# A routing-attention and gated-FFN kernel: the score matmuls contract over 128 rows of the turned tiles instead of 80

## The chip, the cores and the metric

The kernel runs on one core of a Trainium2 chip. The metric is the device time of one execution in microseconds; before the change, three runs gave 336.65, 339.22 and 339.0 us, with a median of 339.0 us. The profile was taken of one execution, whose span from the first to the last instruction is 336.6 us.

## The reference

Four batches, eight heads, 768 positions, head dimension 64. Queries and keys are each assigned to the nearest of 16 centroids of their head; a query attends only to keys of its own cluster. The attention output of all heads, 512 wide, then goes through a gated feed-forward block.

```
q_assign = argmax(q_n @ c_n);  k_assign = argmax(k_n @ c_n)
mask   = q_assign[..., :, None] == k_assign[..., None, :]
scores = where(mask, (q @ k.T) / 8, -1e9)
attn   = softmax(scores);  y = attn @ v
x      = y as (3072, 512)
out    = (sigmoid(x @ w_gate) * (x @ w_val)) @ w_out      # d_ff = 1536
```

## The kernel before

**The turned tiles.** For each head the fp32 keys and queries are cut into an fp16 high part and an fp16 remainder, the low part. They lie side by side as 128 columns of a tile `hl`: columns 0 to 63 the high parts, 64 to 127 the low parts. `hl` is then transposed into a tile `T` of 128 rows by 12 blocks of 128 positions (six blocks of keys, six of queries), in the first batch and in the first pair of heads of the second by TensorE (lines 637, 720 and 796, copied out of PSUM by VectorE or ScalarE), otherwise by a DMA transpose that SyncE's queue issues (line 319). So rows 0 to 63 of `T` hold high parts and rows 64 to 127 low parts of the 64 dimensions.

**Routing.** The logits `lg` (lines 326 and 335) multiply all 128 rows of each block with a centroid matrix. VectorE takes the maximum and writes one-hot rows; these are turned and put into rows 64 to 79 of `T`, over the low parts of 16 dimensions: by VectorE or ScalarE (lines 681, 685 and 769 to 775) or by small DMAs (line 383). Keys get 1 at their cluster; queries get -1920 at every cluster but their own. One matmul over rows 0 to 79 then gives the score and the mask together.

**A step of attention.** There are 96 steps per batch, 384 in all. In `do_scores` a step multiplies one key block (128 columns, stationary) with three query blocks (384 columns, moving) into a PSUM tile `sc` (line 541), and ScalarE takes the exponential of it into `es` (line 546). In `do_av`, two or three steps later, three matmuls of 65 columns multiply `es` with the values (`av`, line 558). The 65th column of the values is 1 and sums the weights. After the last step of a head VectorE and GpSimd normalise, and the result is turned into `xTb`.

**The order.** The order is written out by hand. Each step issues its `sc`, then pieces of the feed-forward block of an earlier half batch (`ffn_run`; gate `g` at line 397, value `v` at line 412, output `o` at line 429, four matmuls to a piece), then the `av` of an older step, then background work due at this step by the table `SCHED`: casts, splits, turns, logits, loads. TensorE executes in that order. The last feed-forward blocks follow the last step, with no attention beside them. Early in the program, and before some steps, dummy matmuls on a zero tile are issued (lines 538 and 604).

`head_steps` makes the slices of `T` that the score matmul uses. It gives `k` as one block and `q` as three; both begin at row 0.

Of the kernel before, what the change touches and what calls it, by code (L numbers as in the profile page):

```python
# [74 lines left out]
def kernel(  # L75
# [443 lines left out]
    def head_steps(b, p, e, halves):  # L519
        t = T[b, 2 * p + e]  # L520
        steps = []
        order = [(j, i) for j in range(NCH) for i in range(len(halves))]
        for j, i in order:
            for c in halves[i : i + 1]:
                steps.append(dict(
                    b=b, p=p, e=e, nq=3 * len(halves), k=t[0:80, j, :], h0=halves[0],
                    q=t[0:80, 6 + 3 * c : 9 + 3 * c, :], j=j, c0=3 * i,
                ))
        steps[0]["first"] = True
        steps[-1]["last"] = True  # L530
        return steps
# [478 lines left out]
    for b in range(B):  # L1010
        xT = xtp.tile([128, NDC, S], HP, tag="xTb", name="xTb")
        key = min(b, 1)
        for i in range(2):
            u = 96 * b + (96 - 6 * 2 * halved(b) if i == 0 else 96)
            lag = SCHED.get(f"lag{key}{i}", 8)
            if b == B - 1 and i:
                break
            at(u + lag, lambda xT=xT, b=b, i=i: ffn_block(xT, 384 * i, 384, b, CH[i]))
        for p, e, c in heads(b):
            for s in head_steps(b, p, e, c):  # L1020
                s["xT"] = xT
                do_scores(s)
                pend.append(s)
                r = step_no[0] - 96 * b
                ns = SCHED.get(f"ns{b}{r // 24}", SCHED.get(f"ns{b}", 500.0))
                ffn_run(ns if b or r >= 48 else 0.0)
                while len(pend) > LA[min(b, 1)]:
                    do_av(pend.pop(0))
                run_bg(step_no[0])
                step_no[0] += 1  # L1030
# [37 lines left out]
```

## Time and profile before

| | |
|---|---|
| three runs | 336.65, 339.22, 339.0 us; median 339.0 us |
| profiled execution, span | 336.6 us; no other time of that execution is listed |
| instructions | 9001, of them 3422 matmuls and 3422 weight loads |
| TensorE busy | 327.1 us (97%) |
| ScalarE, VectorE, GpSimd busy | 236.4, 187.6, 109.3 us |
| score matmuls `sc` | 384, mean 330 ns |
| mean granted TensorE clock | 0.990 |

A busy time of TensorE counts from the start of a matmul to its modelled end, and matmuls overlap, so how much a matmul costs is better read from the distances between starts. The timeline gives these to a hundredth of a microsecond and merges equal instructions that follow one another.

### The profile page before, as it was taken

The numbers are of one execution on the slowest core, as the hardware profiler recorded it, in microseconds if no ns is written. First come the engines' busy times: TensorE is split into PE (matmuls) and PEld (weight loads), VectorE is DVE, ScalarE is ACT, GpSimd is POOL, SyncE is SP. The second block draws the span as 40 slices with busy tenths as digits, with TensorE's granted clock in tenths as the row PEclk, the third lists the DMA queues.
The fourth block names the chain that finished last, engine by engine and source line by source line (L and its number), as shares of the span: only waits on it lengthen the run. The fifth ranks groups of instructions, "written<-read, shape, count | busy, mean of one in ns | idle before, by whom it ended". The sixth has DMA issues, their size and how long they took to land.

```text
span 336.6 us, 9001 instructions
## 1 busy us (share of the span) xinstructions
PE 327.1 (97%) x3422; PEld 210.8 (63%) x3422; DVE 187.6 (56%) x530; ACT 236.4 (70%) x543; POOL 109.3 (32%) x151
## 2 busy tenths in 40 slices
PE   7798999999999999999999999999999999999996
PEld 4686866766666666666556665666556655654654
DVE  6668755796567777465646664466534331340431
ACT  6587987766899888877768776787777876532321
POOL 6668454442254444513242333313201010100000
PEclk9789999999999999999999999999999999999999
DMA  7999989744795969597457755872622022101002
GB/s 205 360 159 129 204 207 188 105 148 91 239 236 106 229 167 237 148 193 196 90 180 168 189 92 116 234 114 49 130 72 47 14 25 74 46 0 64 32 0 95
DMA packets 80523, 45.25 MB, mean 134 GB/s; under 512 B 57376, under 2 KB 77536, under 8 KB 80480
## 3 DMA queue, kind: packets, MB, share of 16 engines
q1 hardware_dynamic: 74400, 39.83, 49.3%
q0 software_dynamic: 5792, 4.72, 9.9%
q8 instruction: 27, 0.44, 0.6%
q14 instruction: 16, 0.13, 0.1%
q10 hardware_dynamic: 288, 0.13, 0.1%
HBM read 28.34 MB, written 6.29 MB: 103 GB/s over the span
## 4 chain that ended last, share of the span: by engine, by line
PE 86%; DMA 5%; DVE 3%; POOL 2%; issue 2%; SPq 1%; ACT 0%; POOLq 0%; DVEq 0%
PE v L412 18%; PE g L397 18%; PE o L429 17%; PE sc L541 17%; PE av L558 9%; DMA qraw<-in_q_dram 3%; PE lg L335 2%; DMA T<-hl 2%; PE lg L326 1%; PE t_ps L720 1%; POOL hl L708 1%; PE o_end L453 1%; POOL wv L198 1%; PE oh_ps L757 1%; DVE hT L417 1%
## 5 line engine op out<-in xcount | busy, mean ns | idle before, releaser
L546 ACT ACTIVATE es<-sc 128x384 f16<-128x384 f32 x384 | 173.5, 492 | 43.2 <-PE sc L541 26.1
L541 PE MATMUL sc<-T 80*128 80x384 f16 x384 | 118.6, 330 | 0.7 <-DVE T L775 0.2
L558 PEld LDWEIGHTS <-es 128*128 128x128 f16 x1152 | 82.6, 98 | 45.6 <-issue 1.5
L558 PE MATMUL av<-va,es 128*128 128x65 f16 x1152 | 98.1, 194 | 0.0
L417 DVE SCALAR_TENSOR_TENSOR hT<-th,v 128x384 f16<-128x384 f32 x96 | 53.1, 553 | 71.7 <-PE av L558 47.4
L397 PE MATMUL g<-xTb,wg 128*128 128x384 f16 x384 | 78.1, 325 | 0.2
L412 PE MATMUL v<-xTb,wv 128*128 128x384 f16 x384 | 78.1, 325 | 0.0
L429 PE MATMUL o<-wo,hT 128*128 128x512 f16 x276 | 68.7, 378 | 0.0
L299 POOL TENSOR_TENSOR xp<-t,rec 128x192 f16<-128x192 f32 (+1 forms) x46 | 29.1, 633 | 116.7 <-DVE rec L296 76.9
L403 ACT ACTIVATE th<-g 128x384 f32<-128x384 f32 x96 | 47.2, 491 | 25.4 <-DVE hT L417 16.2
L397 PEld LDWEIGHTS <-wg 128*128 128x128 f16 x384 | 37.2, 97 | 21.7 <-issue 1.1
L412 PEld LDWEIGHTS <-wv 128*128 128x128 f16 x384 | 37.2, 97 | 21.0 <-issue 0.7
L429 PEld LDWEIGHTS <-hT 128*128 128x128 f16 x276 | 26.8, 97 | 23.5
L541 PEld LDWEIGHTS <-T 80*128 80x128 f16 x384 | 37.3, 97 | 0.8 <-DVE T L775 0.6
L957 POOL TENSOR_TENSOR hl<-kraw,hl 128x384 f16<-128x384 f32 x22 | 20.4, 927 | 34.4 <-DVE hl L956 18.3
L294 DVE TENSOR_TENSOR t<-av,sv 128x195 f32<-128x195 f32 (+1 forms) x46 | 20.1, 436 | 20.4 <-PE av L558 19.7
L957 POOL TENSOR_TENSOR hl<-qraw,hl 128x384 f16<-128x384 f32 x22 | 20.1, 912 | 21.1 <-DVE hl L956 21.1
L438 ACT ACTIVATE ob<-o 128x512 f32<-128x512 f32 x15 | 9.0, 597 | 12.4 <-PE o L429 12.1
L349 DVE TENSOR_TENSOR lgs<-lg,lglo 128x192 f32<-128x192 f32 x22 | 7.8, 356 | 14.6 <-ACT lglo L341 14.2
L436 DVE TENSOR_SCALAR ob<-o 128x512 f32<-128x512 f32 x8 | 5.5, 690 | 16.8 <-PE o L429 16.8
L248 POOL CAST va<-vraw 128x768 f16<-128x768 f32 x16 | 13.5, 848 | 0.2 <-DMA vraw<-in_v_dram 0.2
L335 PE MATMUL lg<-cm,T 128*128 128x32 f16 x264 | 10.0, 177 | 0.4 <-DMA T<-hl 0.4
(112 smaller groups left out, 248.9 us busy)
## 6 DMA issues: line engine op xcount, KB each, us to landing
vraw<-in_v_dram SPq DMA_DIRECT2D x16, 384.0 KB, 5.4
out_dram<-ob SPq DMA_DIRECT2D x23, 256.0 KB, 2.2
kraw<-in_k_dram SPq DMA_DIRECT2D x15, 384.0 KB, 3.9
qraw<-in_q_dram SPq DMA_DIRECT2D x12, 384.0 KB, 4.1
wg<-in_moe_w_gate_dram POOLq DMA_DIRECT2D x4, 384.0 KB, 5.6
wv<-in_moe_w_val_dram POOLq DMA_DIRECT2D x4, 384.0 KB, 5.8
wo<-in_moe_w_out_dram POOLq DMA_DIRECT2D x2, 768.0 KB, 11.2
qraw<-in_q_dram SPq DMA_DIRECT2D x7, 192.0 KB, 6.8
```

What stands on the lines that cost most here:

```text
L294: DVE.tensor_tensor(t[:, 0:nq, :], av, sv, ALU.add)
L299: (eng or POOL).tensor_tensor(x, t[:, 0:nq, 0:64], bcast(rec[:, 0:nq], 64), ALU.mult)
L335: PE.matmul(out=lg[:, bass.ts(c, 32)], lhsT=t[:, c, :], rhs=cm[:, h].rearrange("p s n -> p (s n)"), start=True, stop=True,)
L397: PE.matmul(out=g[:, 0:n], lhsT=wg[fc // WQ][:, dc, fc % WQ, :], rhs=xT[:, dc, t0 : t0 + n], start=(dc == 0), stop=(dc == NDC - 1),)
L403: ACT.activation(th[:, 0:n], g[:, 0:n], AF.Tanh, scale=0.5)
L412: PE.matmul(out=w[:, 0:n], lhsT=wv[fc // WQ][:, dc, fc % WQ, :], rhs=xT[:, dc, t0 : t0 + n], start=(dc == 0), stop=(dc == NDC - 1),)
L417: DVE.scalar_tensor_tensor(hT[:, fc, 0:n], st[0][:, 0:n], 1.0, w[:, 0:n], ALU.add, ALU.mult)
L429: PE.matmul(out=o, lhsT=hT[:, fc, bass.ts(t, 128)], rhs=wo[fc // 6][:, fc % 6, :], start=(fc == 0), stop=(fc == NFC - 1),)
L541: PE.matmul(out=sc.rearrange("p (c t) -> p c t", t=128), lhsT=s["k"], rhs=s["q"], start=True, stop=True,)
L546: ACT.activation(es, sc, AF.Exp, scale=SCALE)
L558: PE.matmul(out=av[:, s["c0"] + i, :], lhsT=s["es"][:, bass.ts(i, 128)], rhs=VA[b, p][:, e, s["j"], :], start=(first and i == 0), stop=(la ...
L957: POOL.tensor_tensor(hl[:, :, 64:128], r, hl[:, :, 0:64], ALU.subtract)
```

## The change

The slices of `T` that the score matmuls read take in all rows. The key block becomes 128 rows by 128 columns instead of 80 by 128, and the query blocks 128 rows by 384 columns instead of 80 by 384. Rows 80 to 127, which are now read too, hold the low parts of dimensions 16 to 63 of keys and queries, so each score gains the product of these low parts.

```diff
         for j, i in order:
             for c in halves[i : i + 1]:
                 steps.append(dict(
-                    b=b, p=p, e=e, nq=3 * len(halves), k=t[0:80, j, :], h0=halves[0],
-                    q=t[0:80, 6 + 3 * c : 9 + 3 * c, :], j=j, c0=3 * i,
+                    b=b, p=p, e=e, nq=3 * len(halves), k=t[:, j, :], h0=halves[0],
+                    q=t[:, 6 + 3 * c : 9 + 3 * c, :], j=j, c0=3 * i,
                 ))
```

The number and the order of the instructions on every engine, and their waits, are the same in both programs.

## The prediction

> **What bounds the kernel now.** The page is read first: the span, the engines, the granted clock, and the chain that ended last.
>
> ```profile
> span 336.6 us, 9001 instructions
> PE 327.1 (97%) x3422; PEld 210.8 (63%) x3422; DVE 187.6 (56%) x530; ACT 236.4 (70%) x543; POOL 109.3 (32%) x151
> PEclk9789999999999999999999999999999999999999
> PE 86%; DMA 5%; DVE 3%; POOL 2%; issue 2%; SPq 1%; ACT 0%; POOLq 0%; DVEq 0%
> PE v L412 18%; PE g L397 18%; PE o L429 17%; PE sc L541 17%; PE av L558 9%; DMA qraw<-in_q_dram 3%; PE lg L335 2%; DMA T<-hl 2%; PE lg L326 1%; PE t_ps L720 1%; POOL hl L708 1%; PE o_end L453 1%; POOL wv L198 1%; PE oh_ps L757 1%; DVE hT L417 1%
> ```
>
> TensorE carries 86% of the chain, the score matmuls 17% of it. The busy share alone would not prove this, because ends of matmuls are modelled; so the second view is the table of busy times over stretches.
>
> ```profile
> core 0: us, PE busy (x) PEld busy (x) DVE busy (x) ACT busy (x) POOL busy (x), PEclk, DMA share, GB/s
> 40.00:290.00 250.00, 248.86 (x2641) 158.67 (x2642) 145.34 (x404) 194.66 (x453) 82.33 (x105) 1.00 0.64 141
> 290.00:330.00 40.00, 40.00 (x229) 22.25 (x228) 13.10 (x25) 12.57 (x25) 0.51 (x1) 1.00 0.07 25
> ```
>
> From 40 to 290 us TensorE is idle for 250.00 - 248.86 = 1.14 us, while ScalarE, the next engine, has 250 - 194.66 = 55 us to spare. A nanosecond that a score matmul gains or loses there goes to the end one for one, and ScalarE, which takes each `sc`, can follow. So the question is only whether a matmul of 80 rows and one of 128 differ in the time that they hold TensorE.
>
> **What the change removes, adds and moves.** It moves nothing: order, count and waits of instructions stay. On 384 weight loads and 384 matmuls the row count goes from 80 to 128. The groups by line give the nearest rows of both kinds.
>
> ```profile
> L541 PE MATMUL sc<-T 80*128 80x384 f16 x384 | 118.6, 330 | 0.7 <-DVE T L775 0.2
> L397 PE MATMUL g<-xTb,wg 128*128 128x384 f16 x384 | 78.1, 325 | 0.2
> L335 PE MATMUL lg<-cm,T 128*128 128x32 f16 x264 | 10.0, 177 | 0.4 <-DMA T<-hl 0.4
> L397 PEld LDWEIGHTS <-wg 128*128 128x128 f16 x384 | 37.2, 97 | 21.7 <-issue 1.1
> L541 PEld LDWEIGHTS <-T 80*128 80x128 f16 x384 | 37.3, 97 | 0.8 <-DVE T L775 0.6
> ```
>
> *Weight loads.* 97 ns with 80 rows, 97 ns with 128: 384 x 0 = 0. They also lie beside the matmul before them (97 ns of load beside some 160 ns of streaming); if that cover were gone nothing would change, since both kinds take the same.
>
> *Waits.* The low rows of `T` are in place before a score is made: the logits of the same tile, among them the 264 of line 335 above, are made of all 128 rows of it, and the one-hot rows, which come last, follow from those logits. No wait is added, nothing new is queued, and no DMA starts earlier or later but by the shift of TensorE itself.
>
> *Matmuls.* The gate's `g` is the changed `sc` in all that the row shows: 128x128 stationary, 128x384 moving. The means (330 against 325) include modelled ends and the first microseconds, so the distances between starts decide. In the timeline of TensorE I took a stretch of steps with feed-forward pieces between them, and the end of attention, where `av` and `v` stand without an `sc`.
>
> ```profile
> 255.76 0.33 PE L541 MATMUL sc<-T 80*128 80x384 f16 x1
> 255.92 0.81 PE L397 MATMUL g<-xTb,wg 128*128 128x384 f16 x4
> ...
> 271.57 0.33 PE L541 MATMUL sc<-T 80*128 80x384 f16 x1
> ...
> 288.23 0.26 PE L558 MATMUL av<-va,es 128*128 128x65 f16 x3
> 288.32 0.81 PE L412 MATMUL v<-xTb,wv 128*128 128x384 f16 x4
> 288.97 0.35 PE L558 MATMUL av<-va,es 128*128 128x65 f16 x6
> 289.15 0.81 PE L397 MATMUL g<-xTb,wg 128*128 128x384 f16 x4
> ...
> 301.50 0.81 PE L412 MATMUL v<-xTb,wv 128*128 128x384 f16 x4
> ```
>
> Price of a feed-forward piece: from 289.15 to 301.50 stand 19 pieces of four, 12.35 / 19 = 0.650 us, so 162.5 ns for one matmul of 128 rows and 384 columns. Price of three `av`: six take 289.15 - 288.97 = 0.18, so 0.09. Between the `sc` at 255.76 and the one at 271.57 lie 21 `sc`, 21 groups of three `av` and 16 pieces: 15.81 - 16 x 0.650 - 21 x 0.09 = 3.52 us, so 168 ns for an `sc` of 80 rows. It holds TensorE 168 - 162.5 = 5 ns longer than a matmul of 128 rows with the same columns. The rows are rounded to 10 ns, so three `av` take 0.085 to 0.095 and the excess is between 0 and 10 ns.
>
> Against the row count as the reason stands a place where `sc` follows logits:
>
> ```profile
> 154.11 0.46 PE L335 MATMUL lg<-cm,T 128*128 128x32 f16 x12
> 154.42 0.32 PE L541 MATMUL sc<-T 80*128 80x384 f16 x1
> 154.58 0.33 PE L412 MATMUL v<-xTb,wv 128*128 128x384 f16 x1
> ```
>
> Here `sc` has 80 rows too, and the next matmul starts after 0.16 us, as behind a `g`. So the extra may belong to the order (an `sc` behind three short `av`), not to the rows; then it stays.
>
> [...]
>
> *Sum.* In full speed stand
>
> ```profile
> L541 PE MATMUL sc<-T x374: 322/327/337, 20.7 to 287.4; 80*128 80x384 f16 x187
> ```
>
> 374 score matmuls between 20 and 290 us. The two ends are 374 x 0 = 0 and 374 x 10 ns = 3.7 us of gain. A loss per matmul is left out, because `g`, `v` and the weight loads of 128 rows show none. I take the middle, 5 ns: the matmul gets the `g` row's price, 374 x 5 = 1.9 us. The profiled execution's 336.6 us would become 334.7 us. That execution lies by the lowest of the three runs (336.65); the median is 339.0, so the time to forecast is 339.0 - 1.9 = **337.1 us**, 0.6% less. One per cent, 3.4 us, is about what a measurement of this kernel tells from no change.
>
> **The rivals.**
>
> *The extra belongs to the order; nothing changes.* For it: the `sc` behind the logits, and equal weight loads. Against it: the `av` to `v` change at 288.32 shows no extra without an `sc` in it. Time: 339.0 us.
>
> *The whole 10 ns goes, or the early half clock gets shorter.* The stretches at the start, as the trace grants the clock:
>
> ```profile
> 5.87:12.69 6.82, 4.65 (x79) 3.38 (x76) 5.02 (x18) 3.40 (x8) 4.69 (x6) 1.00 1.02 346
> 12.69:19.52 6.83, 6.49 (x68) 5.41 (x69) 2.51 (x10) 5.28 (x11) 4.54 (x6) 0.50 1.13 309
> 26.35:33.17 6.82, 5.59 (x105) 4.53 (x104) 5.55 (x19) 5.41 (x13) 5.53 (x9) 1.00 0.92 130
> ```
>
> After a stretch in which TensorE was busy 4.65 of 6.82 us (68%) it ran 6.83 us at 0.50; after one with 5.59 (82%) it did not. If fuller rows counted as more activity, the half-clock stretch could go, worth up to half of 6.83, 3.4 us. Against it: before 12.69 us only a couple of score matmuls run, some 0.3 us of 6.82, so their rows weigh little. The full 10 ns without that gives 339.0 - 3.7 = 335.3 us.
>
> *A second half-clock stretch; slower.* The place is 26 to 33 us, the next emptiest. [...] The price is at most 3.4 us, as above: 339.0 + 3.4 = 342.4 us. For it: the three runs already lie 2.6 us apart, which one such stretch more or less could make. Against it: the change shortens 26 to 33 us by only about ten matmuls times 5 ns. [...]
>
> *Full rows draw the clock down over the whole attention.* The stretch from 290 to 330 us speaks against it: matmuls of 128 rows without a pause, granted clock 1.00. I give it nothing of its own.
>
> *The change doesn't do what it says.* The slices do reach the instructions, and the products of the low parts add a sum whose size no engine's time depends on; what is left of this rival is the first one.
>
> **How the numbers follow.** 45% for the forecast of 337.1 us (its own range 335.5 to 338.5), 36% for no change (339.0, within 337.5 and 340), 12% for the larger gain (335.3 or less), 7% for a half-clock stretch more (342.4). Faster by over 1% means under 335.6: the larger gain's 12% and a little of the forecast's lower edge, 14%. Slower by over 1% means above 342.4: most of the last case, 6%. The rest, 80%, is within 1%. The range from 334.8 to 340.3 us leaves out the last rival, the lowest part of the larger gain and the upper edge of no change. It takes in the lowest run less 1.9 us.
>
> **What the changed profile would show.** If the forecast holds, the timeline of the same steps has about 0.91 - 0.005 us from `sc` to `sc` with one piece between, and the 21 steps that now take 15.81 us take about 15.70. The groups by line give `sc` near 325 ns, its weight load 97. Idle time of TensorE between 40 and 290 us stays near 1 us, and ScalarE's busy time the same 236 us. If 15.81 stays, the order was the reason. If the weight load grows or the clock row shows less than 1.00 after 20 us, the reasoning about equal rows is wrong. What would make the prediction wrong above all is the start: a half-clock stretch more or less moves the time by more than all 374 matmuls do.

## The result and the profile after

The changed kernel takes 337.16 us (median of 20 runs, 334.37 to 338.82), the kernel before 338.79 us (median of 20 runs, 336.49 to 340.37). The ratio is 0.9956 with a 95% interval of 0.9935 to 0.9976: 0.4% faster, about 1.5 us, and clear of no change. The forecast was 337.1 us against 339.0.

The page of the changed kernel, its first lines and two of its groups:

```profile
span 335.1 us, 9001 instructions
PE 325.0 (97%) x3422; PEld 210.5 (63%) x3422; DVE 186.2 (56%) x530; ACT 235.8 (70%) x543; POOL 109.8 (33%) x151
...
L541 PE MATMUL sc<-T 128*128 128x384 f16 x384 | 117.2, 327 | 0.7 <-DVE T L775 0.2
...
L541 PEld LDWEIGHTS <-T 128*128 128x128 f16 x384 | 37.3, 97 | 0.8 <-DVE T L775 0.6
```

The span falls from 336.6 to 335.1 us. The score matmuls now stand with 128 rows; their mean goes from 330 to 327 ns, and the weight load stays at 97 ns. The span is not the whole time: the profiled execution took 337.21 us, 2.1 us more than its span.

The stretch from 40 to 290 us, and the 40 us without attention:

```profile
40.00:290.00 250.00, 248.83 (x2649) 159.81 (x2646) 144.83 (x405) 194.98 (x455) 83.29 (x106) 1.00 0.64 141
290.00:330.00 40.00, 40.00 (x231) 22.40 (x229) 12.98 (x23) 11.84 (x24) 0.00 (x0) 1.00 0.08 30
```

TensorE is idle for 1.17 us in it (1.14 before), with the clock at 1.00. It is as full as it was, and gets through more matmuls (2649 against 2641 in the same 250 us). That is how the bound engine looks here, with each score step 4 ns shorter. The waits behind this idle time changed a little. From 60 to 290 us the profile lists these for TensorE, in the kernel before and then in the changed one (us in total, times, longest):

```profile
PE lg L335 <- DMA T<-hl: 0.4, 1, 0.4
PE t_ps L637 <- DVE T L685: 0.3, 1, 0.3
```

```profile
PE lg L335 <- DMA T<-hl: 0.7, 2, 0.3
```

One wait of 0.3 us is gone and another has come, 0.7 us in sum both times.

The same 21 steps as in the prediction, in the changed kernel's timeline of TensorE:

```profile
254.38 0.33 PE L541 MATMUL sc<-T 128*128 128x384 f16 x1
254.54 0.81 PE L397 MATMUL g<-xTb,wg 128*128 128x384 f16 x4
...
270.11 0.33 PE L541 MATMUL sc<-T 128*128 128x384 f16 x1
```

They take 270.11 - 254.38 = 15.73 us, against 15.81 before: 0.08 / 21 = 4 ns per step. The trace keeps starts in whole nanoseconds: 15.727 against 15.811 us, and behind a score matmul that follows `av` the next matmul starts after 162 ns instead of 166 (medians of some 260 places). Times 384 steps 4 ns are 1.5 us, as much as the two spans differ.

That this comes out so exactly is in part chance. By the starts of the same score matmuls in the two traces, the changed kernel leads by 0.33 us at the 31st, when 4 ns per step would be 0.12, by 1.09 at the 151st, by 0.67 at the 161st, behind its new wait, by 0.81 at the 201st and by 1.55 at the last. From the 201st on this is 4 ns per step; earlier, the two moved waits and the start add and take some tenths of a microsecond, which cancel in these two executions.

### The profile page after: what moved, and what is told of

It is laid out like the page before. It is cut to its first block, busy times and chain, and to the rows that moved or that the text cites. A ratio compares the mean times of both kernels' runs of the same rounds, so it can differ in the third digit from the quotient of the medians.

```text
span 335.1 us, 9001 instructions
## 1 busy us (share of the span) xinstructions
PE 325.0 (97%) x3422; PEld 210.5 (63%) x3422; DVE 186.2 (56%) x530; ACT 235.8 (70%) x543; POOL 109.8 (33%) x151
## 4 chain that ended last, share of the span: by engine, by line
PE 86%; DMA 6%; DVE 2%; POOL 2%; SPq 2%; issue 1%; ACT 0%; POOLq 0%; DVEq 0%; ACTq 0%
PE o L429 18%; PE v L412 17%; PE g L397 17%; PE sc L541 16%; PE av L558 9%; DMA T<-hl 4%; PE lg L335 2%; DMA qraw<-in_q_dram 2%; PE lg L326 1%; PE t_ps L720 1%; POOL hl L708 1%; PE o_end L453 1%; SPq L163 1%; POOL wv L198 1%; DVE T L731 1%
## 5 line engine op out<-in xcount | busy, mean ns | idle before, releaser
L541 PE MATMUL sc<-T 128*128 128x384 f16 x384 | 117.2, 327 | 0.7 <-DVE T L775 0.2
L541 PEld LDWEIGHTS <-T 128*128 128x128 f16 x384 | 37.3, 97 | 0.8 <-DVE T L775 0.6
```

The costliest lines, as they stand in the source:

```text
L541: PE.matmul(out=sc.rearrange("p (c t) -> p c t", t=128), lhsT=s["k"], rhs=s["q"], start=True, stop=True,)
```

## The experiments

What stays open after the result is why a score matmul of 80 rows costs 4 ns more. The theory of the prediction was only "a matmul of 80 rows holds TensorE longer". Three readings of it are told apart below: the price belongs to each matmul of fewer rows; it belongs to certain row counts (those that leave a group of 32 rows half filled, or a whole group unused; the division into groups of 32 is my supposition, which no trace of this case shows); or it is paid where neighbours in TensorE's order differ in their row count. The measure is the length of the same 21 steps, from the timeline; in the rows, the first and the last `sc` of the 21 are shown. It repeats from execution to execution: three executions with 128 rows, two of the changed kernel and one with a fuller start, give 15.727, 15.726 and 15.727 us, and four with 80, 96 and (twice) 112 rows give 15.811 us each. So one execution of each variant is enough here, and a hundredth of a microsecond counts. The time of one execution is no such measure, because the clock at the start differs between executions (see "The start").

**Other row counts for the score: 96, 112 and 64.**

```diff
-                    b=b, p=p, e=e, nq=3 * len(halves), k=t[0:80, j, :], h0=halves[0],
-                    q=t[0:80, 6 + 3 * c : 9 + 3 * c, :], j=j, c0=3 * i,
+                    b=b, p=p, e=e, nq=3 * len(halves), k=t[0:96, j, :], h0=halves[0],
+                    q=t[0:96, 6 + 3 * c : 9 + 3 * c, :], j=j, c0=3 * i,
```

(and the same with 112 and 64)

> The score matmuls contract over 96 rows, three whole groups of 32, in place of 80 or 128. Measure: the same 21 steps late in the third block of steps (from the score matmul before a gate piece to the 21st score matmul after it), 15.81 us with 80 rows and 15.73 us with 128, so 4 ns per step. Theory 'not the full array' (any row count under 128 beside matmuls of 128 costs): 15.81 us. Theory 'broken group' (a row count that doesn't fill its groups of 32 costs): 15.73 us. Weight load 97 ns in both.

> Score matmuls over 112 rows: four groups of 32 are touched, the last one half filled. Theory 'number of groups' (what costs is that a group of 32 is switched off and on): 15.73 us for the 21 steps, as with 128. Theories 'not the full array' and 'broken group': 15.81 us.

With 96 rows, and then with 112, the timelines have

```profile
252.42 0.33 PE L541 MATMUL sc<-T 96*128 96x384 f16 x1
...
268.23 0.33 PE L541 MATMUL sc<-T 96*128 96x384 f16 x1
```

```profile
254.83 0.33 PE L541 MATMUL sc<-T 112*128 112x384 f16 x1
...
270.64 0.33 PE L541 MATMUL sc<-T 112*128 112x384 f16 x1
```

15.81 us both times, exactly as with 80. Whole groups of 32 (96 rows) don't help, and four groups begun (112 rows) don't either. So neither the half-filled group nor the number of groups is the reason, and the gain doesn't grow with the rows: 32 of the 48 added rows bring nothing.

> Score matmuls over the first 64 rows, so the one-hot rows and with them the mask are left out of the scores. Theory 'not the full array': 15.81 us for the 21 steps, as with 80 rows. Theory 'broken group': 15.73 us. [...]

64 rows are another matter. Two steps of that kernel:

```profile
332.00 0.33 PE L541 MATMUL sc<-T 64*128 64x384 f16 x1
332.27 0.82 PE L397 MATMUL g<-xTb,wg 128*128 128x384 f16 x4
332.93 0.26 PE L558 MATMUL av<-va,es 128*128 128x65 f16 x3
333.12 0.33 PE L541 MATMUL sc<-T 64*128 64x384 f16 x1
...
352.13 0.33 PE L541 MATMUL sc<-T 64*128 64x384 f16 x1
```

From the first `av` to `sc` it now takes 0.19 us instead of 0.09, and from `sc` to the next matmul 0.27 instead of 0.16 or 0.17: about 0.1 us on the way in and 0.1 us on the way out. The 21 steps take 20.13 us, 206 ns per step more than with 80 rows, and the span becomes 421.6 us, 85 us more than before. 384 steps at 206 ns make 79 us of it. The clock, which stands at 0.62 on average over the first 49 us of that kernel, may account for the rest, but that was not separated:

```profile
0.00:49.00 49.00, 45.28 (x422) 27.47 (x422) 23.83 (x86) 25.55 (x54) 25.48 (x43) 0.62 0.74 160
```

What in TensorE takes the 0.1 us each way is not shown. 80, 96 and 112 rows don't pay it: their 21 steps take 15.81 us. Row counts between 64 and 80 were not tried.

**Another matmul with 80 rows: the gate.** The score stays at 128 rows.

```diff
-                        out=g[:, 0:n], lhsT=wg[fc // WQ][:, dc, fc % WQ, :],
-                        rhs=xT[:, dc, t0 : t0 + n],
+                        out=g[:, 0:n], lhsT=wg[fc // WQ][0:80, dc, fc % WQ, :],
+                        rhs=xT[0:80, dc, t0 : t0 + n],
```

> Score matmuls over 128 rows as after the change; the gate matmuls instead contract over the first 80 of the 128 rows of each block, so 48 of 128 terms are left out of the gate. Measure: the stretch behind the last attention step, where pieces of four gate and four value matmuls alternate, 19 pieces in 12.35 us now. Theory 'change of rows' (a fixed price of 4 to 7 ns where the row count changes between neighbours): two changes per gate piece, so 10 gate pieces add 0.07 us: 12.42 us, and within a gate piece the second and third distances stay 162 ns. Theory 'price per matmul' (each matmul of 80 rows holds TensorE 4 ns longer): 10 x 4 x 4 ns = 0.16 us: 12.51 us. If 80 rows cost only in the score's place: 12.35 us.

Behind the last attention step, that kernel's timeline has

```profile
288.93 0.82 PE L397 MATMUL g<-xTb,wg 80*128 80x384 f16 x4
289.59 0.33 PE L412 MATMUL v<-xTb,wv 128*128 128x384 f16 x1
...
301.32 0.33 PE L412 MATMUL v<-xTb,wv 128*128 128x384 f16 x1
```

From the gate piece at 288.93 to the value piece at 301.32 lie 19 pieces, 12.39 us instead of 12.35: 0.04 us over ten gate pieces, 4 ns a piece, although each piece has four matmuls of 80 rows. A price per matmul would have given 0.16 us. In whole nanoseconds the extra stands behind the first matmul of a piece, of a gate piece with 80 rows and of a value piece with 128 alike: 166 to 168 ns, and 161 to 162 behind the other three, as expected. So here a run of equal row counts pays once, going in and coming out, and the place of the score is nothing special. The expected 0.07 us was too much: I had taken up to 7 ns for a change in and out, and it is 4.

**The value matmuls with 80 rows, beside a score of 128 and of 80.**

```diff
-                out=av[:, s["c0"] + i, :], lhsT=s["es"][:, bass.ts(i, 128)],
-                rhs=VA[b, p][:, e, s["j"], :],
+                out=av[:, s["c0"] + i, :], lhsT=s["es"][0:80, bass.ts(i, 128)],
+                rhs=VA[b, p][0:80, e, s["j"], :],
```

> Score matmuls over 128 rows; the three value matmuls of a step contract over the first 80 keys of the 128 of each block, so 48 keys of each block are left out of the sums. Measure: the same 21 steps, 15.73 us with all at 128 rows. Theory 'change of rows': each step has one way into 80 rows and one back, 4 ns in all as with the score: 15.81 us. Theory 'price per matmul': 3 x 4 ns per step: 15.98 us.

> Both the score and the value matmuls contract over 80 rows (48 keys of each block are left out of the sums). Neighbours differ in rows only where a feed-forward piece stands between, 16 times in the 21 steps. Theory 'change of rows': 15.73 us + 16 x 4 ns = 15.79 us, and in the five steps without a piece the next value matmul starts 162 ns after the score, not 166. Theory 'price per matmul': 4 x 4 ns per step, 16.07 us.

The first and last `sc` of the 21 steps, with the score at 128 rows and then at 80:

```profile
253.11 0.33 PE L541 MATMUL sc<-T 128*128 128x384 f16 x1
...
268.91 0.33 PE L541 MATMUL sc<-T 128*128 128x384 f16 x1
```

```profile
253.27 0.33 PE L541 MATMUL sc<-T 80*128 80x384 f16 x1
...
269.05 0.33 PE L541 MATMUL sc<-T 80*128 80x384 f16 x1
```

15.80 us: with the score at full rows and the value matmuls at 80, nearly the whole price is back. 15.78 us: with all four at 80 rows it falls again, though four matmuls instead of one now have fewer rows. Per-matmul prices would have given 15.98 and 16.07; a price per matmul in proportion to its columns, 65 against 384, would have given 15.77 and 15.86, and the second is ruled out. Both lengths are near what a price of 4 ns for each in and out gives (15.81 and 15.79). The second sign that was expected is there too: from a score of 80 rows to a value matmul of 80 rows it is 162 ns, and 166 where only one of the two has 80 (medians over the steps without a piece).

**Twice as many changes.** The score at 80 rows, and of the three value matmuls only the middle one.

```diff
-                out=av[:, s["c0"] + i, :], lhsT=s["es"][:, bass.ts(i, 128)],
-                rhs=VA[b, p][:, e, s["j"], :],
+                out=av[:, s["c0"] + i, :], lhsT=s["es"][0 : (80 if i == 1 else 128), bass.ts(i, 128)],
+                rhs=VA[b, p][0 : (80 if i == 1 else 128), e, s["j"], :],
```

> Score matmuls over 80 rows as before, and of the three value matmuls of a step the middle one over the first 80 keys only (48 keys of every block are left out of one third of the sums), so that the row count changes four times per step and not twice. Theory 'change of rows': the price doubles, 15.73 + 21 x 2 x 4 ns = 15.90 us for the 21 steps. Theory 'price of the score matmul alone': 15.81 us.

```profile
256.44 0.33 PE L541 MATMUL sc<-T 80*128 80x384 f16 x1
...
272.35 0.33 PE L541 MATMUL sc<-T 80*128 80x384 f16 x1
```

15.91 us: 0.18 over the 15.73 without any change of rows, where one change in and out per step costs 0.08. The price doubles with the number of changes (0.182 against 0.084 us in whole nanoseconds).

**The time itself.** The changed kernel again, and the score with 112 rows, on one chip and beside the same 29 runs of the kernel before.

> The changed kernel once more, timed beside the next one on one chip. Both theories: 0.9956 of the kernel before within its interval (0.9935 to 0.9976), that is 1.5 us less; the 21 steps take 15.73 us.

> Score matmuls over 112 rows, timed. Theory 'change of rows' (what costs is that neighbours differ, not how many rows there are): no gain at all, 1.000 of the kernel before, although 32 of the 48 added rows are there. Theory 'the gain grows with the rows': two thirds of it, 0.997.

The changed kernel: 336.68 us (12 runs), ratio 0.9963 (0.9937 to 0.9989). With 112 rows: 338.40 us (12 runs), ratio 0.9994 (0.9966 to 1.0021). The interval with 112 rows holds no change and also 0.997, so the time alone doesn't rule out a gain that grows with the rows; the 21 steps, 15.81 against 15.73 us, do, in this trace too.

**The start.** The prediction named the early stretch at half clock as the largest uncertainty. In the changed kernel's profile it stands as before:

```profile
4.40:11.20 6.80, 4.22 (x63) 3.15 (x61) 5.03 (x16) 3.60 (x8) 4.37 (x7) 1.00 0.99 315
11.20:18.00 6.80, 6.36 (x80) 5.21 (x79) 3.15 (x11) 3.72 (x7) 3.67 (x5) 0.50 1.10 343
```

The same kernel, run again for the comparison above, has the second of these stretches at full clock:

```profile
11.20:18.00 6.80, 6.00 (x121) 5.09 (x122) 4.26 (x15) 5.21 (x12) 4.87 (x7) 1.00 1.10 339
```

The clock record of that execution starts at 7.28 us. Over the 6.83 us from there, TensorE is a little less busy than it was ahead of the half clock in the kernel before (4.65 of 6.82 us), and yet the clock stays at 1.00, here and behind it:

```profile
7.28:14.11 6.83, 4.55 (x77) 3.52 (x77) 4.82 (x14) 3.16 (x8) 4.27 (x7) 1.00 1.06 360
```

Four of the 12 runs of the changed kernel show a mean granted clock of 0.999 or more and take 335.2 to 335.4 us; two show 0.989 or 0.990 and take 338.1 and 338.3. Of the kernel before, seven of 29 runs have 0.999 or more, with a median of 336.8 us, and 17 have 0.990 or less, with a median of 339.0. So the runs of one and the same program at 0.999 or more and at 0.990 or less lie 2 to 3 us apart, more than the change gives. Compared at full clock alone the change is worth 336.77 - 335.33 = 1.4 us, near the 1.5 us over all runs.

Filling the gaps of TensorE before that stretch was tried on the changed kernel, with 45 more dummy matmuls:

```diff
-    "ns13": 265, "ns2": 490, "ns3": 500, "dm0": 7, "dm1": 2, "dm2": 5, "dm3": 11, "dm4": 0,
+    "ns13": 265, "ns2": 490, "ns3": 500, "dm0": 7, "dm1": 2, "dm2": 9, "dm3": 18, "dm4": 5,
...
+        if nm in ("h1tu1", "h1lg"):
+            plan(nm, u + off, lambda: dummies(22 if nm == "h1tu1" else 7, 128))
         plan(nm, u + off, lambda: g(*arg, eng))
```

> The changed kernel with 45 more dummy matmuls in the gaps of TensorE between 6 and 12 us. Theory 'the half-clock stretch follows the idle stretch before it, and its place is chance': with the gaps filled the clock stays at 1.00 in every run (mean granted clock 0.999 or more) and the time falls by what the stretch costs, 1.5 to 3 us under the changed kernel, 0.987 to 0.991 of the kernel before. Rival, 'the start is bound by the loads and the engines that split and turn': the clock stays full, but the time falls by under 0.5 us against the changed kernel, or rises because the dummies delay the first steps.

The first row is from the filled kernel; behind it, the stretch from 110 to 150 us of the filled kernel and, in a fence of its own, of the changed kernel as run for this comparison:

```profile
5.20:12.00 6.80, 6.60 (x125) 6.00 (x123) 5.01 (x17) 3.49 (x7) 4.64 (x6) 1.00 1.00 337
...
110.00:150.00 40.00, 38.45 (x424) 24.52 (x421) 25.43 (x73) 32.42 (x79) 16.67 (x22) 1.00 0.89 180
```

```profile
110.00:150.00 40.00, 38.91 (x429) 24.89 (x428) 25.37 (x73) 32.86 (x81) 17.38 (x22) 1.00 0.88 179
```

The clock did most of what was expected: TensorE is busy 6.60 of 6.80 us, and ten of 12 runs show 0.999 or more (four of 12 without the filling), where the expectation was every run. The time did not follow: 336.78 us against 336.68, ratio 0.9971 (0.9943 to 0.9998). The ten runs at full clock have a median of 336.5 us, 1.2 us above those of the changed kernel at full clock. A part of it stands in the rows above: TensorE idles 1.55 us between 110 and 150 us, 1.09 without the filling. So what the runs at full clock gain over the others can't be had by this filling alone. Why the filled start makes the middle wait more is not settled; it is the only filling that was tried.

## Why the prediction was right, point by point

- **The bound.** TensorE is full from 40 to 290 us in both kernels (1.14 and 1.17 us idle), and the 4 ns per step went to the end nearly one for one: 384 x 4 ns = 1.5 us; the medians of 20 runs differ by 1.6 us, the spans of the two profiles by 1.5.
- **Weight loads and waits at nothing.** The weight load takes 97 ns before and after. Single waits of TensorE came and went with the shift in time, but their sum stayed at 0.7 us.
- **The term "168 - 162.5 = 5 ns".** The mechanism that carries the sum was right, its size a little too large: 4 ns measured, so 1.5 us and not 1.9. The error lies in the price of three `av`, 0.09 us from rows rounded to 10 ns. The same working on the changed kernel gives (15.73 - 16 x 0.650 - 21 x 0.09) / 21 = 164 ns, so some 1.5 ns of the 5 were that rounding.
- **How near the number came.** That 337.1 was forecast and 337.16 measured is partly luck. The forecast took 1.9 us from 339.0, the median of three runs; 20 runs of the kernel before have 338.79, and the change gave 1.6. The two errors nearly cancel.
- **The reason behind the term.** "It holds TensorE longer than a matmul of 128 rows" was too coarse. Not the few rows cost but the change of the row count between neighbours: 80, 96 and 112 rows cost alike, four 80-row gate matmuls in a row cost as much as one score, and four changes cost twice what two do. The forecast stands because the edit takes away every such difference that the score made. What in TensorE takes the 4 ns is not shown: no run separates the weight load from the matmul, which have the same row count in all of them.
- **The rival "the extra belongs to the order".** It falls: the order is the same and the extra is gone. The place behind the logits, which spoke for this rival, was read one distance too short. In whole nanoseconds the matmul behind such an `sc` does start after 162 ns in both kernels, but the distance behind that matmul is longer with 80 rows: 165 instead of 162 for a gate matmul, 218 instead of 215 for an `o`, 32 instead of 29 for an `av` (medians). So there the way into 80 rows costs nothing and the way back still costs 3 ns. Why the way in is free behind logits is not shown.
- **The bound of 10 ns, and 64 rows.** The excess at 80 rows was rightly bounded to 10 ns: 4 ns measured. At 64 rows a step takes 206 ns more than at 80 (20.13 against 15.81 us for the 21 steps), so a slice of 64 rows would have been far worse.
- **The half-clock rivals.** The stretch at half clock occurs in both kernels, at 0.50 from 12.69 to 19.52 us before and from 11.20 to 18.00 us after, and the rows of the score have no visible part in it. The prediction set a busy share of 68% ahead of the half clock beside one of 82% without it; the runs show no bound between the two. The changed kernel, run again, was busy 4.55 of 6.83 us (67%) from 7.28 to 14.11 us and kept its full clock there and behind it. "That execution lies by the lowest of the three runs" was wrong: a run's time is 2.1 us more than its span, so the profiled execution of before lay in the middle of the runs. Nothing was built on it, as the gain was taken from the median.

## What to carry to other kernels

Where TensorE is the bound and matmuls of different kinds alternate, let them contract over the same number of rows when the extra rows hold data that does no harm: a score matmul of 128 rows took no longer here than one of 80 (behind it the next matmul started after 162 ns, behind one of 80 rows after 166), and each change of the row count and back cost about 4 ns. Never let one kind fall to 64 rows between others of 128 without looking at the distances between starts: here that cost 206 ns more per step than 80 rows. Effects of this size are read from the distances over many equal steps in the timeline, not from busy time, and not from a few runs whose clock at the start differs.

## What the runs showed that was not expected

- The price of a change of the row count and back is 4.0 ns for a score matmul (0.084 us over 21 steps), the same for 80, 96 and 112 rows beside 128. For three `av`, for four matmuls of 80 rows in a row and with two changes per step it is between 3.3 and 4.3 ns each time.
- At 64 rows beside 128 it is about 0.2 us, half of it going in and half coming out.
- With TensorE busy 4.22 of 6.80 us (62%) and no idle gap longer than 1.64 us, the clock still stood at 0.50 over the next stretch. In another execution of the same program, with 4.55 of 6.83 us (67%), it stayed at 1.00, although it had fallen to 0.50 behind 68% in the kernel before. So the busy share of one such stretch doesn't settle it, and what does stays open.
